# Retention and a squared-ReLU FFN in one kernel: transposing q and k two visits ahead of the scores

## The chip, the cores and the metric

The kernel runs on one core of a Trainium2 chip. The metric is the time on the device in microseconds (us), from the first to the last instruction, as the median of several runs. Five engines work beside each other, each with its own stream of instructions: TensorE (PE for its matmuls, PEld for its weight loads), VectorE (DVE), ScalarE (ACT), GpSimd (POOL) and SyncE (SP), whose stream here holds only transfers. What one engine needs from another it waits for at a semaphore.

## The reference

Two parts are computed, the second from the output of the first. In the retention part, each of 8 batches and 8 heads has 576 positions of 64 numbers. Scores of q against k are weighted by a decay that falls with the distance of two positions, later positions are masked away, and the result is multiplied by v. The FFN then takes 4608 tokens of 512 numbers through 2048 hidden ones.

```python
scores = scale * np.matmul(q, k.transpose(0, 1, 3, 2))       # (8, 8, 576, 576), scale = 1/8
gamma = 1.0 - 2.0 ** (-5.0 - np.arange(H))
rel = pos[:, None] - pos[None, :]
Dmat = np.where(rel >= 0, gamma[:, None, None] ** rel, 0.0)
attn = np.matmul(scores * Dmat, v)
x = attn.transpose(0, 2, 1, 3).reshape(4608, 512)
h = np.maximum(x @ w_in, 0.0)                                # (4608, 2048)
out = h * h @ w_out                                          # (4608, 512)
```

## The kernel before

The retention is done in 40 chunks: each batch has four of 128 positions and one of 64. Between chunks a state `u` is carried, so only scores within a chunk are formed. The FFN's matrix products are done by a scheme of seven products in place of eight (Strassen-Winograd): its sums are made by VectorE. Tokens go through the FFN in blocks of 512; one block is 28 steps (4 groups of hidden columns by 7 products), each of 8 matmuls. These steps are mixed with the chunks. At the end, after the last chunk, the second product of the FFN runs alone (line 893).

One turn of the main loop, a visit, works on two chunks at once: it forms the scores of chunk i and finishes the output of chunk i-1.

```python
for i in range(N_CH + 1):
    if i <= N_EARLY:                        # N_EARLY = 4: the start
        ...
        scale_q(i + 1, nc.gpsimd)
        if i < N_EARLY:
            ...
            turn(i + 1)
    else:
        if i == N_EARLY + 1:
            gone[0] = TOK
        if i + 1 < N_CH:
            scale_q(i + 1, nc.gpsimd)       # q times its decay, in place
        retain_a(i - 1)
        if i < N_TURN:                      # N_TURN = 9
            turn(i)                         # transposes on TensorE, the early chunks only
        ffn(i - 1, 0)                       # some FFN steps
        move(len(moves))                    # whatever copies are left
        if N_TURN <= i + 1 < N_CH:
            flip(i + 1)                     # transposes on VectorE
        retain_b(i - 1)
        if i < N_CH:
            scores(i)
        retain_c(i - 1)
        if N_TURN <= i + 1 < N_CH:
            spread(i + 1)                   # queues the copies of chunk i + 1
        ffn(i - 1, 1)                       # more FFN steps
    if i == 0:
        fetch_raw(2)
    if i + 3 < N_CH:
        load(i + 3)                         # q, k and v
    if 0 < i < N_EARLY:
        fetch_raw(1)
```

q and k come from memory with the position on the partition; the scores need the head's 64 numbers there. For chunks 9 to 39 this is done in two steps. `flip` transposes blocks of 32 by 32 on VectorE, once for k and once for q. `spread` puts 16 small copies (8 for a chunk of 64 positions) in a list, which ScalarE works off: they bring the blocks to their partitions. `move` issues copies from this list.

```python
def flip(i):
    cs = chunks[i][3]
    t = st[i]["flip"] = work2.tile([128, 4, 2, HP, 32], F32, tag="flip", name="flip")
    for j in (1, 0):
        nc.vector.transpose(t[:cs, :, j, :, :], loaded[i][j][:cs].rearrange("s (p e) (d a) -> s (e d) p a", e=2, d=2))  # L390

def spread(i):
    to = new_qk(i)
    for b in range(chunks[i][3] // 32):
        for g in range(4):
            moves.append(lambda b=b, g=g: nc.scalar.copy(          # L396
                to[32 * g:32 * g + 32, :, :, 32 * b:32 * b + 32], st[i]["flip"][32 * b:32 * b + 32, g, :, :, :]))

def scores(i):
    ...
    # 32 small matmuls of kT and qT into sc_ps: L433
    # VectorE: sc_ps times the mask, into the room of kT: L441
    # GpSimd: v times its decay, in place: L443

def scale_q(i, engine):
    ...
    engine.tensor_tensor(t, t, dv[...], op=ALU.mult)               # L373, in the place of q

def ffn(i, half):
    ...                                     # how many steps the tokens finished so far call for
    while steps and count:
        held[0] = half == 0 and count == 1
        move(3)                             # three copies ahead of each step
        step()
        count -= 1
```

An FFN step, as far as it is spoken of: step j of 7 adds into one of three banks of the accumulator memory, a, b or c.

```python
def ffn_in(n, mp, j):
    ...
    if j in OPENS:                          # 0, 1, 2
        sums[to] = ps_f.tile([128, 2, HT], F32, tag="f", name=f"h_{to}")     # three buffers
    ...                                     # 8 matmuls: L614
    if j == 0:
        nc.scalar.copy(p1, p)                                                # bank a, L624
    elif j == 1:
        nc.vector.tensor_tensor(u2, p, p1, op=ALU.add)                       # bank b, L626
    elif j == 2:
        nc.vector.tensor_tensor(p15, p, p1, op=ALU.add)                      # bank c, L628
    elif j == 3:
        nc.scalar.activation(g["A11"], p, AF.Relu)                           # bank a, L630
        nc.gpsimd.tensor_tensor(g["A11"], g["A11"], g["A11"], op=ALU.mult)   # L631
    elif j == 4:
        nc.vector.tensor_tensor(g["A22"], p, p15, op=ALU.add)                # bank b, L633
        square(g["A22"])                                                     # L621
    elif j == 5:
        nc.vector.tensor_tensor(g["S3"], p, u2, op=ALU.add)                  # bank c, L637
        square(g["S3"])
    else:
        nc.vector.tensor_tensor(g["A12"], p, p1, op=ALU.add)                 # bank b, L640
        square(g["A12"])
        queue.extend(g_sums(n, mp))                                          # four sums, L552 to L555, a transfer
```

The steps also work off, piece by piece, the conversion of the weights of the second product: five VectorE instructions (L207 to L225) and two of ScalarE (L215, L216) for each of 16 pieces, and sums over them.

Buffers: q has three, k and v have four, `flip` and `qk` have two each.

Of the kernel before, what the change touches and what calls it, by code (L numbers as in the profile page):

```python
# [9 lines left out]
F32 = mybir.dt.float32  # L10
# [5 lines left out]
C = 128  # L16
# [24 lines left out]
def kernel(  # L41
# [33 lines left out]
    nc = tc.nc  # L75
    ctx.enter_context(tc.manual_schedule())

    B, H, S, D = q.shape
    HP = H // 2
# [12 lines left out]
    N_CH = len(chunks)  # L92
# [5 lines left out]
    first = ExitStack()  # L98
    only = first.enter_context(tc.tile_pool(name="only", bufs=1))
    ld3 = first.enter_context(tc.tile_pool(name="ld3", bufs=3))  # L100
    ld4 = first.enter_context(tc.tile_pool(name="ld4", bufs=4))
    work = first.enter_context(tc.tile_pool(name="work", bufs=1))
    work2 = first.enter_context(tc.tile_pool(name="work2", bufs=2))
    ps_x = first.enter_context(tc.tile_pool(name="ps_x", bufs=1, space=PS))
    ps_t = first.enter_context(tc.tile_pool(name="ps_t", bufs=1, space=PS))
# [4 lines left out]
    W = [const.tile([128, N_MQ * NP * 128], F32, name=f"w{j}") for j in range(NP)]  # L110
# [17 lines left out]
    loaded = {}  # L128
    N_EARLY = TOK // C

    def load(i):
        b, ci, c0, cs = chunks[i]
        got = {name: pool.tile([128, H, D], F32, tag=name, name=f"{name}_ld") for name, pool in (("q", ld3), ("k", ld4), ("v", ld4))}
        if i == 0:
            nc.sync.dma_start(dv, decays)
        for name, src in (("q", q), ("k", k), ("v", v)):
            t = got[name]

            issue = nc.scalar if i == 0 and name != "q" else nc.sync
            at = src[b, :, c0:c0 + cs, :].rearrange("h s d -> s h d")  # L140
            if name == "v":
                issue.dma_start(t[:cs], at)
            else:

                issue.dma_start(t[:cs, 0:H // 2, :], at[:, 0:H // 2, :])
                for e in range(2):
                    issue.dma_start(t[:cs, H // 2 + e::2, :], at[:, H // 2 + 1 - e::2, :])
        loaded[i] = [got["q"], got["k"], got["v"]]

# [39 lines left out]
    def fetch_w(j):  # L191
        if j < len(pieces) and wide:
            nc.sync.dma_start(raw_of(j).bitcast(I64).rearrange("p (c f) -> p c f", c=N_DM), piece_src(j))
# [88 lines left out]
    def fetch_raw(count):  # L282

        for _ in range(count):
            if n_raw[0] < min(N_W1, n_made[0] + N_RAW):
                fetch_w(n_raw[0])
                n_raw[0] += 1
# [25 lines left out]
    def convert(count):  # L313
        for _ in range(count):
            f = next(w_in_steps, None)
            f and f()
# [1 line left out]
    dv = only.tile([128, H, 2 * NCH], F32, name="dv")  # L318
    exp_bias = const.tile([128, 1], F32, name="exp_bias")
    nc.gpsimd.memset(exp_bias, -896.0 * 2.0 ** 23)  # L320
    idle = only.tile([128, 128], F32, name="idle")
    nc.vector.memset(idle, 1.0)
    load(0)
    load(1)
    fetch_raw(1)
    load(2)

    ident = only.tile([128, 128], F32, name="ident")
    make_identity(nc, ident)

    msk = only.tile([128, 1, 1, CH], F32, name="msk")
# [1 line left out]
    for half in range(2):  # L333
        at = slice(CH * half, CH * half + CH)
# [8 lines left out]
    st = {i: {} for i in range(N_CH)}  # L343
# [11 lines left out]
    def rows(half, n=64):  # L355
        return slice(64 * half, 64 * half + n)
# [13 lines left out]
    def scale_q(i, engine):  # L370
        ci, cs = chunks[i][1], chunks[i][3]
        t = loaded[i][0][:cs]
        engine.tensor_tensor(t, t, dv[:cs, :, NCH + ci:NCH + ci + 1].to_broadcast([cs, H, D]), op=ALU.mult)  # L373
# [4 lines left out]
    N_TURN = 9  # L378
    moves = []

    def new_qk(i):
        t = work2.tile([128, 2, HP, C], F32, tag="qk", name="qk")
        st[i]["qT"], st[i]["kT"] = t[:, 0, :, :], t[:, 1, :, :]
        return t

# [4 lines that stand above are left out]
            nc.vector.transpose(t[:cs, :, j, :, :], loaded[i][j][:cs].rearrange("s (p e) (d a) -> s (e d) p a", e=2, d=2))  # L390

    def spread(i):
        to = new_qk(i)
        for b in range(chunks[i][3] // 32):
            for g in range(4):
                moves.append(lambda b=b, g=g: nc.scalar.copy(  # L396
                    to[32 * g:32 * g + 32, :, :, 32 * b:32 * b + 32], st[i]["flip"][32 * b:32 * b + 32, g, :, :, :]))

    def move(count):
        for f in moves[:count]:  # L400
            f()
        del moves[:count]

    def turn(i):

        cs = chunks[i][3]
        n_h = cs // CH
        p = ps_t.tile([128, 2, 512], F32, tag="t", name="t_ps").rearrange("p h (j d t) -> p h j d t", j=2, d=HP)
        for j in (1, 0):
            for hp in range(HP):  # L410
                for h in range(n_h):
                    nc.tensor.transpose(p[:, h, j, hp, :], loaded[i][j][rows(h), 2 * hp:2 * hp + 2, :],
                                        ident[rows(h), rows(h)])
        to = new_qk(i)[:, :, :, :cs].rearrange("p j d (h t) -> p j d h t", h=n_h)
        nc.scalar.copy(to[:, 1].rearrange("p d h t -> p h d t"), p[:, :n_h, 1, :, :])
        nc.vector.tensor_copy(to[:, 0].rearrange("p d h t -> p h d t"), p[:, :n_h, 0, :, :])
# [279 lines left out]
    def ffn(i, half):  # L696

        gone[0] += chunks[max(0, min(i, N_CH - 1))][3] / 2
        if steps and steps[0][0] == 0:

            move(6)
            for f in (step, lambda: convert(6)) if half else (lambda: convert(6), step):
                f()
            if half and steps and steps[0][0] == 0:
                step()
                convert(6)
            return
        if not behind:
            behind.append((gone[0] - HALF, done[0]))
        points = behind + [p for p in PACE if p[0] > behind[0][0]]  # L710
        want = points[-1][1]
        for (x0, y0), (x1, y1) in zip(points, points[1:]):
            if gone[0] < x1:
                want = y0 + (y1 - y0) * (gone[0] - x0) / (x1 - x0)
                break
        count = max(1, int(want) - done[0])
        while steps and count:
            held[0] = half == 0 and count == 1
            move(3)
            step()  # L720
            count -= 1
        held[0] = False
# [15 lines left out]
    for i in range(N_CH + 1):  # L738
        if i <= N_EARLY:

            if i == 1:
                convert(2)
            elif i == 2:
                convert(5)
            if i >= 1:
                retain_a(i - 1)
                if i < 3:
                    warm(4, False)
                else:
                    convert(1)  # L750
                    first_in(2 * i - 5, (0,))
                    convert(5)
                retain_b(i - 1)
                if i < 3:
                    warm(4, False)
                retain_c(i - 1)
            convert((0, 1, 1, 0, 1)[i])
            if i == N_EARLY:
# [3 lines that stand above are left out]
            if i == 2:  # L762
                convert(5)
                first_in(0, (0,))
            elif i == 3:
                convert(1)
                first_in(2, (0,))
                convert(5)
            elif i == N_EARLY:
                convert(5)  # L770
                step()
                convert(6)
            scale_q(i + 1, nc.gpsimd)
            if i < N_EARLY:
                if i < 2:
                    warm(6, False)
                turn(i + 1)
        else:
            if i == N_EARLY + 1:
                gone[0] = TOK  # L780
            if i + 1 < N_CH:
                scale_q(i + 1, nc.gpsimd)
            retain_a(i - 1)
            if i < N_TURN:
                turn(i)
            ffn(i - 1, 0)
            move(len(moves))
            if N_TURN <= i + 1 < N_CH:
                flip(i + 1)
            retain_b(i - 1)  # L790
            if i < N_CH:
                scores(i)
            retain_c(i - 1)
            if N_TURN <= i + 1 < N_CH:
                spread(i + 1)
            ffn(i - 1, 1)
        if i == 0:
            fetch_raw(2)
        if i + 3 < N_CH:
            load(i + 3)  # L800
        if 0 < i < N_EARLY:
            fetch_raw(1)
    assert n_next[0] == N_BLK
    first.close()

# [165 lines left out]
    for k in range(N_K + 1):  # L971
# [4 lines left out]
        for e in range(3):  # L976
# [8 lines left out]
            f = next(steps_0, None)  # L985
# [50 lines left out]
```

## Time and profile before

| what | value |
|---|---|
| median of 3 runs | 1007.1 us (1004.7 to 1008.47) |
| span of the profiled run | 1007.7 us |
| TensorE matmuls busy | 966.5 us, 96% |
| TensorE weight loads busy | 861.4 us, 85% |
| VectorE busy | 786.1 us, 78% |
| ScalarE busy | 351.3 us, 35% |
| GpSimd busy | 128.7 us, 13% |
| mean granted TensorE clock | 0.983 |

A busy time is the time in which at least one instruction of the engine was under way. A line such as L396 is a line of the kernel's code; a row of the profile gives the line, the engine, the operation, what is written and read, and how often. The idle time in front of an instruction is put down to the event that came last before it. The granted clock is given as a share of full speed. The chunks run until about 553 us, the FFN's remaining first-product steps until about 605 us, and the second product alone to the end.

### The profile page before, as it was taken

To read this page: it belongs to the slowest core of one execution; us is meant where nothing else is said; L and a number is where in the kernel's file an instruction comes from. 1 tells how busy PE (TensorE), PEld (TensorE's weight loads), DVE (VectorE), ACT (ScalarE), POOL (GpSimd) and SP (SyncE) were. 2 spreads that over 40 slices of the span, in tenths; PEclk is the share of its full clock that TensorE was granted. 3 is DMA by queue.
4 is the path that set the end of the run, shared out by engine and by line. 5 is a ranking of instruction groups with operands and counts; after the bars stand their busy time and mean duration, and the time that the engine had idled before them with its cause. 6 is when DMAs were issued, how large, how long until landed. Compare 5 with 4: busy or idle time off the path is not lost. (4 is left out here: it accounts for less than half of the span.)

```text
span 1007.7 us, 24117 instructions
## 1 busy us (share of the span) xinstructions
PE 966.5 (96%) x10092; PEld 861.4 (85%) x10092; DVE 786.1 (78%) x1458; ACT 351.3 (35%) x871; POOL 128.7 (13%) x121
## 2 busy tenths in 40 slices
PE   7899989999999899989989999999999999999998
PEld 6645768788878778877878889999999999999998
DVE  3789787768998799998977677777777677777766
ACT  3454575674665656746562110000000000000000
POOL 3211212312123131212120000000000000000000
PEclk7999999999999899999989999999999999999999
DMA  8883657655798589669437998684865757565351
GB/s 196 239 226 115 171 163 208 180 154 178 204 296 236 147 247 268 211 180 297 135 126 299 394 419 320 250 293 144 287 210 187 272 176 255 187 241 209 127 210 43
DMA packets 185037, 219.19 MB, mean 218 GB/s; under 512 B 118624, under 2 KB 135008, under 8 KB 175968
## 3 DMA queue, kind: packets, MB, share of 16 engines
q1 hardware_dynamic: 182816, 217.13, 66.3%
q8 instruction: 79, 1.29, 0.5%
q10 hardware_dynamic: 2112, 0.52, 0.2%
q14 instruction: 30, 0.25, 0.1%
HBM read 128.23 MB, written 89.39 MB: 216 GB/s over the span
## 5 line engine op out<-in xcount | busy, mean ns | idle before, releaser
L396 ACT COPY qk<-flip 32x256 f32<-32x256 f32 x440 | 177.1, 402 | 34.2 <-DVE flip L390 27.8
L614 PE MATMUL h_b<-room,w 128*128 128x256 f32 x736 | 179.4, 387 | 1.9 <-DVE room L539 1.6
L614 PEld LDWEIGHTS h_b<-room,w 128*128 128x128 f32 x736 | 139.6, 193 | 23.3 <-issue 2.1
L893 PE MATMUL o_b<-w,room 128*128 128x128 f32 x1168 | 144.5, 275 | 1.5 <-DVE room L844 1.5
L893 PEld LDWEIGHTS o_b<-w,room 128*128 128x128 f32 x1168 | 137.2, 192 | 1.7 <-DVE room L844 1.7
L893 PE MATMUL o_c<-w,room 128*128 128x128 f32 x1008 | 123.0, 275 | 0.0
L893 PEld LDWEIGHTS o_c<-w,room 128*128 128x128 f32 x1008 | 117.7, 192 | 0.0
L614 PE MATMUL h_c<-room,w 128*128 128x256 f32 x480 | 116.6, 386 | 0.0
L614 PE MATMUL h_a<-room,w 128*128 128x256 f32 x448 | 109.8, 389 | 3.1 <-ACT room L624 3.1
L907 ACT COPY r<-o_a 128x128 f32<-128x128 f32 x53 | 14.1, 265 | 273.3 <-PE o_a L893 242.5
L614 PEld LDWEIGHTS h_c<-room,w 128*128 128x128 f32 x480 | 91.8, 193 | 13.2
L614 PEld LDWEIGHTS h_a<-room,w 128*128 128x128 f32 x448 | 84.9, 193 | 15.7 <-ACT room L624 3.5
L893 PE MATMUL o_a<-w,a 128*128 128x128 f32 x688 | 85.6, 275 | 0.0
L631 POOL TENSOR_TENSOR room<-room 128x512 f32<-128x512 f32 x32 | 35.4, 1105 | 387.9 <-ACT room L630 368.5
L893 PEld LDWEIGHTS o_a<-w,a 128*128 128x128 f32 x688 | 81.2, 192 | 0.1
L621 DVE SCALAR_TENSOR_TENSOR room<-room 128x512 f32<-128x512 f32 x96 | 75.5, 786 | 3.3
L578 PE MATMUL h_ps<-room,w 128*128 128x512 f32 (+1 forms) x160 | 58.7, 515 | 3.5 <-DVE w L225 2.6
L373 POOL TENSOR_TENSOR q_ld<-q_ld,dv 128x512 f32<-128x512 f32 (+1 forms) x39 | 47.2, 1210 | 76.5 <-DMA q_ld<-in_q_dram 70.1
L455 PEld LDWEIGHTS x_ps<-qk,v_ld 64*64 64x64 f32 x1152 | 42.0, 141 | 15.3 <-issue 13.7
L433 PE MATMUL sc_ps<-qk 64*64 64x64 f32 x1152 | 35.5, 233 | 19.5 <-ACT qk L396 16.1
L455 PE MATMUL x_ps<-qk,v_ld 64*64 64x64 f32 x1152 | 51.1, 230 | 3.0 <-DVE qk L441 2.0
L633 DVE TENSOR_TENSOR room<-h_b,room 128x512 f32<-128x512 f32 x32 | 22.1, 690 | 39.0 <-PE h_b L614 38.9
(111 smaller groups left out, 1419.8 us busy)
## 6 DMA issues: line engine op xcount, KB each, us to landing
g_dram<-room SPq DMA_DIRECT2D x32, 1792.0 KB, 7.8
a<-g_dram SPq DMA_DIRECT2D x43, 1024.0 KB, 7.3
room<-g_dram SPq DMA_DIRECT2D x20, 1024.0 KB, 6.3
w<-w_dram SPq DMA_DIRECT2D x7, 1792.0 KB, 12.9
out_dram<-room SPq DMA_DIRECT2D x17, 512.0 KB, 3.3
w<-in_moe_w_in_dram SPq DMA_DIRECT2D x16, 512.0 KB, 5.7
w<-in_moe_w_out_dram SPq DMA_DIRECT2D x16, 512.0 KB, 3.8
v_ld<-in_v_dram SPq DMA_DIRECT2D x31, 256.0 KB, 4.0
```

The source lines that it names most:

```text
L373: engine.tensor_tensor(t, t, dv[:cs, :, NCH + ci:NCH + ci + 1].to_broadcast([cs, H, D]), op=ALU.mult)
L396: moves.append(lambda b=b, g=g: nc.scalar.copy(to[32 * g:32 * g + 32, :, :, 32 * b:32 * b + 32], st[i]["flip"][32 * b:32 * b + 32, g, :, : ...
L433: nc.tensor.matmul(sc[e][rows(h), hp, :], lhsT=kT[rows(e), hp, t], rhs=qT[rows(e), hp, t], start=True, stop=True, skip_group_check=True)
L455: own.append(lambda hp=hp, e=e, b=b: nc.tensor.matmul(x_at(hp, b, h), lhsT=s["vs"][rows(h), 2 * hp + b, :], rhs=s["ret"][rows(h), e, hp, : ...
L578: nc.tensor.matmul(p.rearrange("p h t -> p (h t)"), lhsT=w[:, c, :], rhs=xT[0][:, c, lo * HT:hi * HT], start=(c == 0), stop=(c == N_DM - 1))
L614: nc.tensor.matmul(p[:, mm, :], lhsT=w[:, c, :], rhs=xs[n][right][:, c, :], start=(j in OPENS and mm == 0 and c == 0), stop=(j in CLOSES a ...
L621: nc.vector.scalar_tensor_tensor(t, t, 0.0, t, op0=ALU.max, op1=ALU.mult)
L631: nc.gpsimd.tensor_tensor(g["A11"], g["A11"], g["A11"], op=ALU.mult)
L633: nc.vector.tensor_tensor(g["A22"], p, p15, op=ALU.add)
L893: nc.tensor.matmul(p, lhsT=s["lefts"][left][:, m, :], rhs=w_out[j][:, m, WO_SLOT[right], :], start=(i in OPENS and m == 0), stop=(i in CLO ...
L907: nc.scalar.copy(r[:, 0, 0:128], p)
```

## The change

The copies should no longer be issued close before the scores that need them, nor close behind the transposes that they read. So the whole chain is pulled apart: in visit i, q and k of chunk i+4 are loaded (v stays at i+3), GpSimd scales q of chunk i+3, VectorE transposes chunk i+2, and the copies of chunk i+1 are queued; what is left of the copies of chunk i is issued at the visit's start, ahead of the FFN steps instead of behind them. The transposes stand behind the scores and the mask of chunk i. The first chunks go over to the new order between visits 5 and 9.

This needs one more buffer of k (five) and one more of `qk` (three). Their room is found by letting two small constant tiles, `idle` and `ident`, lie in a part of the weight buffer `W[6]` that is not used at that time.

```diff
+    ld5 = first.enter_context(tc.tile_pool(name="ld5", bufs=5))
+    work3 = first.enter_context(tc.tile_pool(name="work3", bufs=3))
 ...
-    def load(i):
+    def load(i, names="qkv"):
 ...
-        for name, src in (("q", q), ("k", k), ("v", v)):
-            t = got[name]
+        got = loaded.setdefault(i, [None] * 3)
+        for name, pool, src in (("q", ld3, q), ("k", ld5, k), ("v", ld4, v)):
+            if name not in names:
+                continue
+            t = got["qkv".index(name)] = pool.tile([128, H, D], F32, tag=name, name=f"{name}_ld")
 ...
-    idle = only.tile([128, 128], F32, name="idle")
+    idle, ident = (W[6][:, at:at + 128] for at in (2688, 2816))
 ...
     def new_qk(i):
-        t = work2.tile([128, 2, HP, C], F32, tag="qk", name="qk")
+        t = work3.tile([128, 2, HP, C], F32, tag="qk", name="qk")
 ...
-    def move(count):
-        for f in moves[:count]:
-            f()
-        del moves[:count]
+    def move(count, i=N_CH):
+        while moves and count and moves[0][0] <= i:
+            nc.scalar.copy(*moves.pop(0)[1:])
+            count -= 1
 ...
-            if i + 1 < N_CH:
-                scale_q(i + 1, nc.gpsimd)
             retain_a(i - 1)
             if i < N_TURN:
                 turn(i)
+            move(C, i)
             ffn(i - 1, 0)
-            move(len(moves))
-            if N_TURN <= i + 1 < N_CH:
-                flip(i + 1)
             retain_b(i - 1)
             if i < N_CH:
                 scores(i)
             retain_c(i - 1)
             if N_TURN <= i + 1 < N_CH:
                 spread(i + 1)
+            if N_TURN <= i + 2 < N_CH:
+                flip(i + 2)
             ffn(i - 1, 1)
         if i == 0:
             fetch_raw(2)
-        if i + 3 < N_CH:
+        if i < N_TURN - 1:
             load(i + 3)
+        else:
+            if i == N_TURN - 1:
+                load(i + 3, "qk")
+            if i + 4 < N_CH:
+                load(i + 4, "qk")
+            if i + 3 < N_CH:
+                load(i + 3, "v")
         if 0 < i < N_EARLY:
             fetch_raw(1)
+        if i > N_EARLY:
+            for j in range(i + 1 + 2 * (i > N_EARLY + 1), min(i + 4, N_CH)):
+                scale_q(j, nc.gpsimd)
```

More of the change, by code (lines that the diff above doesn't have):

```diff
@@ L129 @@
     N_EARLY = TOK // C
-    def load(i):
+    def load(i, names="qkv"):
         b, ci, c0, cs = chunks[i]
-        got = {name: pool.tile([128, H, D], F32, tag=name, name=f"{name}_ld") for name, pool in (("q", ld3), ("k", ld4), ("v", ld4))}
         if i == 0:
             nc.sync.dma_start(dv, decays)
-        for name, src in (("q", q), ("k", k), ("v", v)):
-            t = got[name]
+        got = loaded.setdefault(i, [None] * 3)
[3 more added lines that the diff above has]
+            t = got["qkv".index(name)] = pool.tile([128, H, D], F32, tag=name, name=f"{name}_ld")
             issue = nc.scalar if i == 0 and name != "q" else nc.sync
@@ L147, in load @@
                     issue.dma_start(t[:cs, H // 2 + e::2, :], at[:, H // 2 + 1 - e::2, :])
-        loaded[i] = [got["q"], got["k"], got["v"]]
     pieces = [(0, m, e) for m in range(N_M) for e in range(2)]
@@ L326 @@
     load(2)
-    ident = only.tile([128, 128], F32, name="ident")
     make_identity(nc, ident)
@@ L392, in spread @@
     def spread(i):
-        to = new_qk(i)
+        t, to = st[i]["flip"], new_qk(i)
         for b in range(chunks[i][3] // 32):
             for g in range(4):
-                moves.append(lambda b=b, g=g: nc.scalar.copy(
-                    to[32 * g:32 * g + 32, :, :, 32 * b:32 * b + 32], st[i]["flip"][32 * b:32 * b + 32, g, :, :, :]))
-    def move(count):
-        for f in moves[:count]:
-            f()
-        del moves[:count]
+                moves.append((i, to[32 * g:32 * g + 32, :, :, 32 * b:32 * b + 32], t[32 * b:32 * b + 32, g, :, :, :]))
+    def move(count, i=N_CH):
+        while moves and count and moves[0][0] <= i:
+            nc.scalar.copy(*moves.pop(0)[1:])
+            count -= 1
     def turn(i):
```

## The prediction

> **What bounds the kernel now.** I read the busy rows first, then TensorE's own waits, then stretches of the time, and last the instructions around two of the waits. The page's busy rows:
>
> ```profile
> PE 966.5 (96%) x10092; PEld 861.4 (85%) x10092; DVE 786.1 (78%) x1458; ACT 351.3 (35%) x871; POOL 128.7 (13%) x121
> ...
> PEclk7999999999999899999989999999999999999999
> ```
>
> TensorE is the bound over the span: it lacks only 1007.7 - 966.5 = 41 us. The change can win only idle time of TensorE, or time at which its clock was lowered. The second line shows that the clock dips below full speed in a few slices of the middle. What TensorE waited for, in the whole span:
>
> ```profile
> PE sc_ps L433 <- ACT qk L396: 16.1, 19, 3.6
> PE sc_ps L433 <- DVE qk L416: 3.4, 3, 1.4
> PE h_a L614 <- ACT room L624: 3.1, 1, 3.1
> ...
> PE x_ps L455 <- DVE qk L441: 2.0, 1, 2.0
> PE h_b L614 <- DVE room L539: 1.6, 1, 1.6
> ```
>
> The columns are us in total, times and the longest. The largest entry is just what the change aims at: the scores (L433) waiting for ScalarE's copies (L396) of the transposed q and k, 16.1 us in 19 waits. By stretch (us, then busy time of each engine, granted clock, DMA):
>
> ```profile
> 120.00:240.00 120.00, 114.22 (x1423) 96.66 (x1422) 94.04 (x144) 73.70 (x181) 27.34 (x24) 0.99 0.63 178
> 240.00:510.00 270.00, 252.94 (x2930) 213.28 (x2928) 242.60 (x390) 164.59 (x392) 63.76 (x55) 0.97 0.73 221
> 510.00:600.00 90.00, 89.62 (x652) 77.56 (x651) 64.63 (x104) 21.53 (x49) 8.49 (x8) 0.98 0.78 304
> 600.00:1007.70 407.70, 402.85 (x3568) 401.39 (x3566) 299.84 (x679) 33.76 (x126) 1.04 (x1) 1.00 0.61 216
> ```
>
> TensorE's idle time where the changed code runs is 5.8 + 17.1 + 0.4 = 23 us, and the waits named above for this part (16.1 + 3.1 + 2.0 + 1.6) explain all of it. From 240 to 510 VectorE is busy 242.6 of 270 us, 90%: it is nearly a second bound. After 600 nothing of the change runs.
>
> The clock matters too. Two pairs of slices of 10 us around the longest waits, same columns:
>
> ```profile
> 320.00:330.00 10.00, 7.52 (x52) 6.16 (x50) 9.18 (x14) 8.52 (x20) 4.76 (x4) 0.94 0.99 263
> 330.00:340.00 10.00, 9.95 (x100) 8.31 (x101) 5.78 (x11) 5.37 (x15) 0.00 (x0) 0.72 0.48 120
> ...
> 500.00:510.00 10.00, 6.08 (x111) 5.07 (x109) 7.31 (x13) 5.46 (x13) 3.06 (x3) 0.82 0.47 177
> 510.00:520.00 10.00, 10.00 (x69) 8.29 (x68) 6.35 (x12) 6.46 (x16) 0.00 (x0) 0.84 0.03 10
> ```
>
> In slices of 1 us the clock is either 1.00 or 0.50. It is 0.50 for about 3.2 us from 138, 6.7 us from 329, 3.4 us from 438, 3.3 us from 476 and 6.4 us from 507, each time after TensorE had stood still for about 2 us or more. Half of these 23 us, less the part in which TensorE stood anyway, is about 11 us lost, beside the 23 us of idling.
>
> Why the copies are late is seen on ScalarE's own timeline (start, duration, instruction) at two of these places:
>
> ```profile
> 434.73 1.23 ACT L396 COPY qk<-flip 32x256 f32<-32x256 f32 x3 [5.67 <-DVE flip L390]
> 435.99 0.59 ACT L624 COPY room<-h_a 128x512 f32<-128x512 f32 x1
> ...
> 503.30 0.72 ACT L215 ACTIVATE w<-w,exp_bias 128x512 uint32<-128x512 uint32 x1 [2.66 <-DVE w L207]
> 503.93 0.65 ACT L216 ACTIVATE w<-w 128x512 f32<-128x512 uint32 x1
> 504.60 1.23 ACT L396 COPY qk<-flip 32x256 f32<-32x256 f32 x3
> 505.85 0.60 ACT L630 ACTIVATE room<-h_a 128x512 f32<-128x512 f32 x1
> 506.47 1.65 ACT L396 COPY qk<-flip 32x256 f32<-32x256 f32 x4
> ```
>
> At 434.7 ScalarE had stood 5.67 us for the transpose, which VectorE, running late, reached only then; the copy L624 queued behind it, and TensorE's next h_a waited 3.1 us for that. At 503.3 ScalarE stood for VectorE's weight conversion with seven copies still behind it in the queue, and the scores waited 3.6 us. ScalarE is only a third busy, so its rate is not the trouble: it inherits VectorE's lateness in order.
>
> **What the skill says.** The Trainium skill, "TensorE: Matmul & The Clock Gate", section on the HAM clock gate: the clock falls to half when the array has idled for about a window of 3.4 us, and needs about as long to come back. The trace agrees in the two levels and in the 3.2 to 6.7 us of half clock, but here 2.1 to 2.5 us of standing still were enough (before 138 and 329), while 1.6 us (at 297.5) was not. The same page, in its table and under "Architectural detail", says ScalarE and VectorE take their queues strictly in order; the two places above show it. "SBUF — State Buffer", section "Who interferes with whom": a VectorE instruction with two SBUF inputs and a GpSimd one that reads SBUF block each other. At 425.2 us VectorE's L539 took 1.54 us beside GpSimd's L373 of 1.50 us, against usual 0.68 and 1.06; so GpSimd's scaling isn't free to VectorE wherever it is put, but its amount does not change.
>
> **The change part by part.** No instruction of the steady part is added or removed: 31 chunks are still transposed by 62 VectorE instructions (0.70 and 0.66 us) and spread by 440 ScalarE copies of 0.402 us, and 40 scalings stay. What moves is order.
>
> (1) The transpose of chunk i+1 stood in visit i after the first half of the FFN steps, and its copies followed right behind retain_c, about 1.7 us of TensorE's time later (304.6 to 306.3 us in one visit of the timeline). Now it is issued a whole visit earlier, and a visit lasts about (540 - 100)/31 = 14 us. ScalarE should hardly ever stand for it: the 27.8 us (15 times) that it stood for L390 go, and with them the 3.1 us of h_a.
>
> (2) The last of the 16 copies were dealt out in threes among the FFN steps before the scores. Now the remainder is flushed ahead of those steps: half a visit, some 3.5 steps of 8 x 0.236 = 1.89 us, so 6.6 us of margin. The longest wait was 3.6 us, so I expect at most 1 of the 16.1 us to stay.
>
> (3) VectorE's mask (L441) now stands ahead of the transposes instead of behind: 1.36 us earlier. Of the 2.0 us wait I give it 1.
>
> (4) With no wait above 2 us left of this kind, most of the half clock goes: 9 of 11 us.
>
> Gains: 15 + 2.6 + 1 + 9 = 27.6 us.
>
> (5) Given back: from 240 to 510 TensorE without these losses (17 us idle, about 9 us clock) would need 244 us. VectorE has 390 instructions there. Where it is saturated (17 to 19 instructions in 9.9 us) one takes some 0.57 us, that is 222 us; by its busy time it needs 243. So it would be 91 to nearly 100% loaded, and the FFN's tightest link lets it lag only about one step (bank b is read after step 4 and written again in step 6). I put 6 us of new waits there, clock included.
>
> (6) The flush puts up to 7 x 0.402 = 2.8 us of copies ahead of one FFN copy per visit: 1 us in all, since that copy has two steps (3.8 us) of room.
>
> (7) The switch from one scheme to the other: chunks 9 and 10 are loaded only in the visits before they are transposed, and VectorE stands in order for load, scaling and transpose. Landing takes up to 10.3 us for q and GpSimd waited 60 us for q before 120 us. 1.5 us.
>
> Net: 27.6 - 8.5 = 19 us, 1007 - 19 = **988 us**.
>
> **Rivals.** *VectorE becomes the bound*: 390 instructions in 270 us speak for it, and its idle time there is only 27 us, 14 of it waiting for h_b (L633). Then the 26 us of TensorE's losses there shrink to perhaps 8 recovered, plus 5 before 240: about 994 to 997. Against it speaks that in the kernel before, at 90%, TensorE waited for VectorE's FFN work only 1.8 us. *Everything is recovered*: 23 + 11 us, at no cost: 973; for it that VectorE's instructions overlap when dense (starts 0.60 us apart for 0.68 us). *The transfer takes the wait's place*: transposes in order behind q that hasn't landed would stop VectorE and so everything; the time would be 1005 to 1015. In the steady part a load now has about two visits (28 us) against 10.3 us, and before, GpSimd's wait for q from 230 to 520 was 4.6 us, once; so this is only a start-up cost.
>
> **Range and chances.** The middle lies between the first two rivals, nearer to the balance of (1) to (7). 979 is two thirds of full recovery plus a little luck with the clock; 1000 is VectorE taking most of it. The 2% line is 987 us, close to the middle: faster by over 2% 0.43, within 2% 0.54, slower by over 2% 0.03.
>
> **What would show it.** Right: the scores' wait for L396 under 2 us, ScalarE's wait for L390 near zero, no half clock between 240 and 510, TensorE's busy share of that phase near 97%, VectorE's near 95% with its waits for h_b shrunk, and new small waits of h_b and h_c for VectorE. Wrong: VectorE idle for flip's inputs (q_ld) beyond visit 10, or new waits of TensorE for VectorE above 12 us with fresh half-clock stretches. If the clock doesn't recover though the waits go, part (4) is wrong.

## The result and the profile after

| what | before | changed |
|---|---|---|
| median | 1006.99 us | 996.49 us (993.29 to 998.64) |
| ratio | | 0.9895, 95% interval 0.9862 to 0.9928 |
| span of the profiled run | 1007.7 us | 994.4 us |
| TensorE's waits, 120 to 600 us | 23.4 us | 16.8 us |
| clock below full, 120 to 600 us | 11.9 us | 6.8 us |

The change brings 10.5 us, 1.05%; 19 us were predicted. The last row adds up, over slices of 10 us, the share of the clock that was missing, as full-clock time; 1.1 us of the 11.9 and 0.7 us of the 6.8 fell while TensorE stood, so those count in both rows.

The page of the changed kernel; lines are numbered anew (L403 is L396 of before, L616 is L614, L635 is L633):

```profile
PE 960.5 (97%) x10092; PEld 855.8 (86%) x10092; DVE 788.7 (79%) x1458; ACT 350.2 (35%) x871; POOL 131.9 (13%) x121
...
L616 PE MATMUL h_b<-room,w 128*128 128x256 f32 x736 | 181.9, 391 | 10.6 <-DVE room L635 4.3
L403 ACT COPY qk<-flip 32x256 f32<-32x256 f32 x440 | 177.0, 402 | 6.3
```

The same 440 copies take the same 177 us, but ScalarE stood only 6.3 us in front of them and none of it for a transpose. In front of the FFN's matmuls into bank b, TensorE now stood 10.6 us, for VectorE. Its waits from 120 to 600 us (total, times, longest) in the changed kernel:

```profile
PE h_b L616 <- DVE room L635: 4.0, 3, 1.4
PE sc_ps L435 <- ACT qk L403: 3.5, 6, 1.1
PE h_b L616 <- DVE room L628: 3.5, 1, 3.5
PE x_ps L457 <- ACT u_sb L495: 3.1, 4, 2.1
PE h_b L616 <- DVE room L541: 1.6, 1, 1.6
PE x_ps L457 <- DVE qk L443: 0.8, 1, 0.8
```

The wait that the change is for went from 16.1 to 3.5 us, and the 3.1 us for bank a are gone. New are 7.5 us for L635 and L628, which read FFN sums out of bank b, and 3.1 us (0.4 before) for L495: a copy of two numbers per partition on ScalarE at the end of retain_b, behind which retain_c's first matmul must stand. The stretches:

```profile
120.00:240.00 120.00, 117.15 (x1444) 98.58 (x1442) 99.30 (x153) 73.64 (x182) 28.89 (x25) 1.00 0.64 175
240.00:510.00 270.00, 256.27 (x2984) 215.93 (x2984) 248.36 (x395) 171.00 (x411) 64.11 (x54) 0.97 0.73 219
510.00:600.00 90.00, 89.63 (x649) 78.57 (x648) 66.58 (x103) 14.41 (x32) 9.98 (x9) 1.00 0.90 348
```

VectorE is now busy 248 of 270 us in the middle, 92%, with 395 instructions in place of 390. The clock there is 0.97 as before.

What a new wait looks like: VectorE of the changed kernel (start, duration, instruction) around the longest.

```profile
424.92 0.68 DVE L443 TENSOR_TENSOR qk<-sc_ps,msk 128x512 f32<-128x512 f32 x1
425.52 0.69 DVE L392 STREAM_TRANSPOSE flip<-k_ld 64x512 f32<-64x512 f32 x1
426.14 0.66 DVE L392 STREAM_TRANSPOSE flip<-q_ld 64x512 f32<-64x512 f32 x1
426.74 0.64 DVE L543 TENSOR_TENSOR room<-room 128x512 f32<-128x512 f32 x1
427.31 0.67 DVE L555 TENSOR_TENSOR room<-room 128x512 f32<-128x512 f32 x1
427.90 1.25 DVE L247 TENSOR_TENSOR w<-w,w 128x256 f32<-128x256 f32 x1
429.19 1.17 DVE L248 TENSOR_TENSOR w<-w,w 128x256 f32<-128x256 f32 x1
430.28 0.68 DVE L628 TENSOR_TENSOR room<-h_b,room 128x512 f32<-128x512 f32 x1
```

VectorE has no gap: mask, transposes, a sum over x, an FFN sum, two sums over weights, and only then L628, for which TensorE had been ready since about 427.5. L247 and L248 took 1.25 and 1.17 us instead of about 0.42 (the median of their eight executions each at this shape). GpSimd in the same microseconds, changed kernel:

```profile
427.67 1.21 POOL L633 TENSOR_TENSOR room<-room 128x512 f32<-128x512 f32 x1 [8.48 <-ACT room L632]
428.84 1.23 POOL L375 TENSOR_TENSOR q_ld<-q_ld,dv 128x512 f32<-128x512 f32 x1
430.04 1.23 POOL L445 TENSOR_TENSOR v_ld<-v_ld,dv 128x512 f32<-128x512 f32 x1
```

The Trainium skill's "SBUF — State Buffer", section "Who interferes with whom", says that a VectorE instruction with two SBUF inputs and a GpSimd instruction that reads SBUF block each other. The two slow VectorE sums agree: they have two such inputs and stand beside these three instructions. TensorE in slices of 1 us (us, busy, clock, DMA) shows the price of the wait:

```profile
428.00:429.00 1.00, 0.00 (x0) 1.00 0.00 0
429.00:430.00 1.00, 0.00 (x0) 0.80 0.00 0
430.00:431.00 1.00, 0.00 (x0) 0.50 0.00 0
431.00:432.00 1.00, 0.99 (x2) 0.50 0.00 0
432.00:433.00 1.00, 1.00 (x4) 0.50 0.00 0
433.00:434.00 1.00, 1.00 (x4) 0.50 0.00 0
434.00:435.00 1.00, 1.00 (x3) 0.50 0.40 152
```

After 3.5 us of standing it runs at half clock: 3 or 4 matmuls touch a slice; at full clock, from 437 to 439 us, 6 do. The slice from 430 to 440 us has a mean clock of 0.68, so this lasts until about 436.4: 5.4 us of running at half speed, 2.7 us lost.

The profiled spans differ by 13.3 us, the medians by 10.5. The profiled execution of the kernel before took 1009.39 us, more than any of its four runs. Part of the excess lies at the start, where nothing of the new order runs yet: between 10 and 20 us the profiled run of before had a granted clock of 0.59, that of the changed kernel 1.00, and its chunk 4 was masked at 46.2 instead of 48.0 us. The rest of the difference about adds up: 6.6 us less waiting and 5.1 us less missing clock, 0.4 us of it counted twice.

### The profile page after: what moved, and what is told of

Read it like the earlier page. It is cut to its first block, busy times and chain, and to the rows that moved or that the text cites. A ratio compares the mean times of both kernels' runs of the same rounds, so it can differ in the third digit from the quotient of the medians.

```text
span 994.4 us, 24115 instructions
## 1 busy us (share of the span) xinstructions
PE 960.5 (97%) x10092; PEld 855.8 (86%) x10092; DVE 788.7 (79%) x1458; ACT 350.2 (35%) x871; POOL 131.9 (13%) x121
## 5 line engine op out<-in xcount | busy, mean ns | idle before, releaser
L616 PE MATMUL h_b<-room,w 128*128 128x256 f32 x736 | 181.9, 391 | 10.6 <-DVE room L635 4.3
L403 ACT COPY qk<-flip 32x256 f32<-32x256 f32 x440 | 177.0, 402 | 6.3
L616 PEld LDWEIGHTS h_b<-room,w 128*128 128x128 f32 x736 | 139.9, 193 | 33.2 <-DVE room L635 6.1
L616 PE MATMUL h_c<-room,w 128*128 128x256 f32 x480 | 115.9, 385 | 0.0
L917 ACT COPY r<-o_a 128x128 f32<-128x128 f32 x53 | 14.1, 266 | 272.5 <-PE o_a L903 241.9
L616 PE MATMUL h_a<-room,w 128*128 128x256 f32 x448 | 107.6, 383 | 0.0
L616 PEld LDWEIGHTS h_c<-room,w 128*128 128x128 f32 x480 | 91.9, 193 | 13.6 <-DVE room L642 0.3
L616 PEld LDWEIGHTS h_a<-room,w 128*128 128x128 f32 x448 | 83.7, 190 | 12.1 <-ACT room L626 0.3
L633 POOL TENSOR_TENSOR room<-room 128x512 f32<-128x512 f32 x32 | 36.9, 1152 | 370.4 <-ACT room L632 264.5
L623 DVE SCALAR_TENSOR_TENSOR room<-room 128x512 f32<-128x512 f32 x96 | 72.3, 753 | 3.3
L580 PEld LDWEIGHTS h_ps<-room,w 128*128 128x128 f32 x160 | 29.2, 190 | 25.0 <-issue 20.4
L445 POOL TENSOR_TENSOR v_ld<-v_ld,dv 128x512 f32<-128x512 f32 (+1 forms) x40 | 47.5, 1187 | 13.6 <-DMA v_ld<-in_v_dram 5.9
```

What stands on the lines that cost most here:

```text
L403: nc.scalar.copy(*moves.pop(0)[1:])
L445: nc.gpsimd.tensor_tensor(vs[:cs], vs[:cs], dv[:cs, :, ci:ci + 1].to_broadcast([cs, H, D]), op=ALU.mult)
L580: nc.tensor.matmul(p.rearrange("p h t -> p (h t)"), lhsT=w[:, c, :], rhs=xT[0][:, c, lo * HT:hi * HT], start=(c == 0), stop=(c == N_DM - 1))
L616: nc.tensor.matmul(p[:, mm, :], lhsT=w[:, c, :], rhs=xs[n][right][:, c, :], start=(j in OPENS and mm == 0 and c == 0), stop=(j in CLOSES a ...
L623: nc.vector.scalar_tensor_tensor(t, t, 0.0, t, op0=ALU.max, op1=ALU.mult)
L917: nc.scalar.copy(r[:, 0, 0:128], p)
```

## Experiments

Theory: ScalarE's copies were late because, in order, ScalarE inherits VectorE's lateness; the change frees the scores of that, and TensorE then meets VectorE itself, which has too little slack to give 19 us. Rivals: one of the two moves (transposes earlier, copies earlier) does it all and the other is idle; or what is left comes from ScalarE's order or from transfers, not from VectorE's load. All ratios are to the kernel before, with their 95% intervals; that of the changed kernel is 0.9895. Each edit is one to the changed kernel unless said otherwise. Waits come from one profiled execution of a kernel, which can lie some us off the median (996.09 us for the changed kernel, 1006.11 for e2, 998.83 for e9, 994.78 for e11).

### The two moves apart

e1_flush_only, an edit to the kernel before:

```diff
+            move(len(moves))
             ffn(i - 1, 0)
-            move(len(moves))
```

> The kernel before with one part of the change: what is left of the copies is issued ahead of the first half of the FFN steps instead of behind it; transposes, loads and scaling stay where they were. Theory A (copies are late because ScalarE stands for late transposes and conversions of VectorE; margin before the scores is what counts): the scores' wait for the copies falls from 16 us to about 5 us, but ScalarE's wait for the transposes (27.8 us) stays and pushes the FFN copy of bank a, so TensorE's wait for that one stays at 3 us or grows; time 999 to 1003 us. Rival B (only the distance between transpose and copies counts): nothing gained, 1005 to 1009 us.

e2_flip_only:

```diff
-            move(C, i)
             ffn(i - 1, 0)
+            move(C, i)
```

> The changed kernel with one part undone: what is left of the copies is issued behind the first half of the FFN steps again, as before; transposes stay two visits ahead. Theory A: ScalarE hardly waits for transposes, but the scores still come close behind the last copies, which queue behind weight conversions: the scores' wait is 6 to 9 us and the time 999 to 1003 us. Rival B (distance from the transposes is all): as the changed kernel, 995 to 998 us, with the scores' wait at 4 us or less.

Measured: copies early alone 1000.65 us, ratio 0.9942 (0.9922 to 0.9961); transposes early alone 1002.35 us, 0.9964 (0.9949 to 0.9979). TensorE's and then ScalarE's waits with the copies early alone:

```profile
PE sc_ps L433 <- ACT qk L396: 6.0, 7, 2.2
...
PE h_a L614 <- ACT room L624: 2.7, 2, 2.5
```

```profile
ACT qk L396 <- DVE flip L390: 38.7, 18, 5.1
```

and the same two with the transposes early alone:

```profile
PE sc_ps L435 <- ACT qk L403: 15.6, 19, 4.7
```

```profile
ACT w L218 <- DVE w L210: 14.6, 9, 3.8
```

```profile
500.19 0.72 ACT L218 ACTIVATE w<-w,exp_bias 128x512 uint32<-128x512 uint32 x1 [3.84 <-DVE w L210]
```

With the copies early alone the scores wait 10 us less, but ScalarE stands longer for the transposes (27.8 before, 38.7 now) and the FFN's bank a still waits. With the transposes early alone ScalarE never stands for them, yet the scores wait as long as before, since the copies still come last and queue behind the weight conversion L218, which stands 14.6 us for VectorE: at 500.19 us it had stood 3.84 us with seven copies behind it, and there the scores waited 4.7 us. So rival B falls: the distance from the transposes alone leaves the scores' wait where it was. Theory A had that wait too small as well, at 6 to 9 us; the time is as it had it. Each move alone is worth 0.4 to 0.6%, together 1.05%: about a sum.

### VectorE lightened, in both kernels

e3_light_before (in the kernel before) and e4_light_after (in the changed kernel) leave out 32 of VectorE's instructions of the second weight's conversion, so the second weights have neither their exponent nor their sign:

```diff
+        if j >= N_W1:
+            four = five = lambda: None
         return [one, two, beside, three, four, five]
```

> The kernel before with VectorE lightened: two of five VectorE instructions of each of the 16 pieces of the second weight's conversion are left out (scaling by the exponent and the sign), 32 instructions, about 25 us of VectorE, nearly all between 240 and 510 us; the second weights are then not converted rightly. Theory (in the changed kernel VectorE is the new bound, in the kernel before ScalarE's late copies are): the kernel before gains only through less lateness of VectorE, about 3 to 8 us: 999 to 1004 us. Rival (VectorE isn't a bound in either): under 3 us.

> The changed kernel with the same 32 VectorE instructions left out. Theory (VectorE is the new bound): TensorE's direct waits for VectorE between 120 and 600 us fall from 10 us to under 4 us, stretches of half clock go too, and the time falls by 8 to 13 us, to 983 to 988 us, more than what the kernel before gains from the same cut. Rival (what is left are late copies on ScalarE and transfers, not VectorE): less than 4 us gained, 993 to 997 us.

Measured: the kernel before gains 5.9 us, to 1001.31 (0.9946, 0.9928 to 0.9965), the changed one 11.7 us, to 984.83 (0.9777, 0.9761 to 0.9792). Stretch and waits of the lightened changed kernel:

```profile
240.00:510.00 270.00, 260.82 (x3078) 220.85 (x3077) 237.07 (x383) 174.76 (x420) 60.46 (x54) 1.00 0.76 228
```

```profile
PE sc_ps L437 <- ACT qk L405: 2.8, 4, 1.1
PE h_b L618 <- DVE room L637: 2.7, 2, 1.5
PE x_ps L459 <- ACT u_sb L497: 2.1, 4, 1.2
PE h_b L618 <- DVE room L543: 1.6, 1, 1.6
...
PE h_c L618 <- DVE room L632: 0.5, 1, 0.5
```

The scores' wait in the lightened kernel before:

```profile
PE sc_ps L435 <- ACT qk L398: 14.7, 17, 2.4
```

The same cut is worth twice as much once the copies are out of the way, and the clock stays full from 120 to 600 us. In the lightened kernel before, the scores still wait 14.7 us for the copies and the clock still lacks 11.9 us: there ScalarE's order is the limit, which less VectorE work doesn't cure. The direct waits for VectorE fell from 10.2 to 4.8 us, where under 4 were expected; a wait of 1.3 us in the second product, which here begins before 600 us, is not in the 4.8. That VectorE's load is what the changed kernel runs into is shown by this pair.

### The order of VectorE's work

e5_dealt_flips:

```diff
-            nc.vector.transpose(t[...], loaded[i][j][...])
+            later.append(lambda j=j, src=loaded[i][j]: nc.vector.transpose(t[...], src[...]))
 ...
             move(3)
             step()
+            if later:
+                later.pop(0)()
 ...
             retain_c(i - 1)
+            while later:
+                later.pop(0)()
```

> The changed kernel with the two transposes of a visit dealt out: one behind each of the next two FFN steps instead of both at once behind the mask; VectorE's work is the same, only its bursts are shorter. Theory (VectorE's total load limits, and bursts make it bite): TensorE's direct waits for VectorE fall from 10 us to 6 to 8 us; time 991 to 995 us. Rival (only the total load counts, the order of VectorE's work does not): 995 to 998 us.

e7_mask_behind:

```diff
+            if N_TURN <= i + 2 < N_CH:
+                flip(i + 2)
             retain_b(i - 1)
             if i < N_CH:
                 scores(i)
             retain_c(i - 1)
 ...
-            if N_TURN <= i + 2 < N_CH:
-                flip(i + 2)
```

> The changed kernel with the transposes ahead of retain_b, the scores and the mask again, where they stood before, but still two visits ahead. If the mask's place matters as the prediction's part (3) says, TensorE's wait for the mask (0.8 us) rises by 1 to 2 us and the time to 997 to 999 us; if it doesn't, 995 to 998 us, the same as the changed kernel.

Measured: dealt out 1000.09 us, 0.9944 (0.9924 to 0.9964), a miss for both theories, as its median is 3.6 us above that of the changed kernel, though the two intervals just overlap; mask behind 999.09 us, 0.9924 (0.9900 to 0.9948), whose interval overlaps that of the changed kernel. With dealt-out transposes TensorE's direct waits for VectorE rose from 11.5 to 12.8 us (from 100 to 600 us) and that for the tiny copy from 3.1 to 4.7 us. Shorter bursts don't help here. A likely reason, not shown, is that VectorE has hardly a gap to put them in, so that a transpose between two steps delays the next read-out of a bank as well. With the mask behind, TensorE's wait for it is 2.5 us in place of 0.8, as part (3) has it.

### GpSimd's share

e8_no_scaling leaves GpSimd's scaling of q out for chunks 10 to 39, so their scores lack the decay by position:

```diff
-                scale_q(j, nc.gpsimd)
+                if j <= N_TURN:
+                    scale_q(j, nc.gpsimd)
```

> The changed kernel without GpSimd's scaling of q for chunks 10 to 39 (30 instructions of 1.2 us left out; the scores of these chunks lack the decay). VectorE's instruction count is the same. If instructions of VectorE with two inputs are held up by GpSimd's, VectorE's busy time for the same work falls by up to 10 us, its waits with it, and the time is 990 to 994 us; if GpSimd's work costs VectorE nothing, 995 to 998 us.

Measured: 991.68 us, 0.9857 (0.9829 to 0.9885). From 240 to 510 us, VectorE's instructions add up to 272.5 us in 395 in the changed kernel (0.690 us each) and 270.1 us in 405 here (0.667 each): the same 405 at 0.690 would be 279 us, so about 9 us of VectorE's time there went with GpSimd's scaling of q. Most of it shows in rows whose two inputs lie in SBUF, as here (changed kernel, then e8):

```profile
L554 DVE TENSOR_TENSOR room<-room 128x512 f32<-128x512 f32 x17 | 13.4, 786 | 0.0
...
L554 DVE TENSOR_TENSOR room<-room 128x512 f32<-128x512 f32 x17 | 11.6, 684 | 0.0
```

L635, which reads one of its inputs from a bank, took 687 and 686 ns, and the transposes of k 696 and 697. Taking the scaling away is worth about 5 us, with intervals that overlap in part.

### Work moved to ScalarE

e6_a12_scalar moves one of three squares per group to ScalarE, as a ReLU and a square one step later; e9_early_fence puts retain_b and the tiny copy one FFN step earlier; e10_fence_a12 has both; e12_fence_a12_late issues the square another step later; e11_fence_a11 has the early tiny copy and moves GpSimd's square to ScalarE.

```diff
             nc.vector.tensor_tensor(g["A12"], p, p1, op=ALU.add)
-            square(g["A12"])
-            queue.extend(g_sums(n, mp))
+            todo = g_sums(n, mp)
+            second, t = todo[1], g["A12"]      # e12: todo[2]
+            def with_square():
+                second()
+                nc.scalar.activation(t, t, AF.Relu)
+                nc.scalar.activation(t, t, AF.Square)
+            todo[1] = with_square              # e12: todo[2]
+            queue.extend(todo)
```

```diff
-            ffn(i - 1, 0)
-            retain_b(i - 1)
+            early = [lambda: retain_b(i - 1)]
+            ffn(i - 1, 0, early)               # issued ahead of the last step of this half
+            while early:
+                early.pop()()
```

```diff
-            nc.gpsimd.tensor_tensor(g["A11"], g["A11"], g["A11"], op=ALU.mult)
+            nc.scalar.activation(g["A11"], g["A11"], AF.Square)
```

> The changed kernel with one of the three squares per group of FFN steps moved from VectorE (0.6 to 0.8 us) to two ScalarE instructions (about 1.2 us), dealt out one step later; 32 squares, some 17 of them between 240 and 510 us, so about 11 us less of VectorE there and 20 us more of ScalarE, which has 99 us free. Theory (VectorE is the bound): 988 to 992 us. Rival (ScalarE's queue in order is as tight as VectorE): the gain is eaten by later copies, the scores' wait rises over 6 us, 995 to 1000 us.

> The changed kernel with retain_b, and the tiny ScalarE copy behind it that retain_c waits for, one FFN step earlier, ahead of the last step of the first half; the rest is unchanged. In the changed kernel TensorE waited 3.1 us for that copy, in the kernel with one square on ScalarE 7.8 us. Theory (it is ScalarE's order that costs here): this wait falls below 1 us and the time to 991 to 994 us. Rival (TensorE then merely meets VectorE's lateness one step later): 995 to 998 us.

> The early tiny copy together with one square per group moved from VectorE to ScalarE. Theory (VectorE's load is the bound, and the moved square lost its gain only at the tiny copy): 986 to 991 us, TensorE's waits for VectorE under 6 us and for the tiny copy under 1 us. Rival (ScalarE's queue in order costs as much elsewhere, at the copies for the scores): 995 to 1000 us.

> The early tiny copy together with GpSimd's square (one per group) moved to ScalarE, right behind the ReLU that it follows. VectorE's own work is the same, GpSimd loses about 17 of 54 instructions between 240 and 510 us. If GpSimd's reads hold up VectorE's instructions with two inputs, VectorE's busy time falls by 3 to 5 us there and the time to 989 to 992 us; if not, or if ScalarE's 0.6 us more per group cost as much, it is as with the early copy alone.

> The early tiny copy together with one square per group on ScalarE, the square issued one FFN step later still. In the kernel with the square one step earlier ScalarE stood 5.9 us for VectorE's sum that the square reads (990 to 995 us measured there). Theory (ScalarE's standing in order for VectorE is what is left of that kernel's loss): ScalarE's wait for that sum falls below 2 us, the waits for the tiny copy and the copies for the scores fall from 6.4 to under 4 us, 988 to 992 us. Rival (VectorE's last sum of the group, which reads the square, now has to wait for ScalarE and takes the gain back): VectorE waits for the square for 3 us or more, 992 to 996 us.

| run | us | ratio (95% interval) | waits for VectorE | for the tiny copy | for the copies of q and k |
|---|---|---|---|---|---|
| changed kernel | 996.49 | 0.9895 (0.9862 to 0.9928) | 10.2 | 3.1 | 3.5 |
| e6, square on ScalarE | 999.47 | 0.9937 (0.9914 to 0.9960) | 4.3 | 7.8 | 4.8 |
| e9, early tiny copy | 995.35 | 0.9888 (0.9866 to 0.9910) | 9.5 | 1.5 | 2.7 |
| e10, both | 992.65 | 0.9861 (0.9838 to 0.9883) | 4.0 | 2.7 | 3.7 |
| e12, both, square later | 993.00 | 0.9866 (0.9845 to 0.9887) | 4.2 | 2.4 | 2.6 |
| e11, early tiny copy, GpSimd's square | 998.65 | 0.9909 (0.9890 to 0.9929) | 4.0 | 4.7 | 3.2 |

The last three columns are TensorE's waits in us from 120 to 600 us. e6 came out in its rival's range: VectorE's waits shrank as they should, but ScalarE's queue grew and its next link gave way: not so much the copies for the scores, as the rival had it, as the tiny copy:

```profile
PE x_ps L457 <- ACT u_sb L495: 7.8, 7, 2.9
PE sc_ps L435 <- ACT qk L403: 4.8, 8, 1.1
```

The early tiny copy alone does little, since VectorE's waits stay, as e9's rival had it. Together they give 992.65 us. The prediction for e10 was 986 to 991. In e12 ScalarE no longer stood for the sum that the square reads (5.9 us in e10), and VectorE's last sum of the group waited only 0.7 us for the square; yet the time is the same, so that standing had cost nothing. What both have against them is at another place: VectorE's L628, which adds a copy that ScalarE makes, stood 11.4 us for ScalarE in e10 and 11.7 in e12, 2.2 in the changed kernel; what that cost was not tested. In e11 VectorE's mean instruction was 0.684 us against 0.690, so these squares had hardly held VectorE up, and the wait for the tiny copy was 4.7 us. TensorE's waits for VectorE fell to 4.0 us in its profiled execution, but that was the fastest of the five, and its median is above that of e9, within the intervals.

Two versions thus stand at 993 us, below both kernels; their intervals overlap that of the changed kernel a little, so a gain over it of 3 to 4 us is likely, not certain.

## Why the prediction was right, and where its size was not

- **The whole.** The range of 979 to 1000 us held (its lower end takes back 28 of the 34 us, four fifths and not the two thirds that it is called); the middle was 8.5 us too fast. Of the signs that were named for being right, ScalarE no longer stood for the transposes, TensorE had new waits for VectorE (one of them 3.5 us long), and VectorE was 92% busy, near the 95 named. The others did not come: the scores waited 3.5 us and not under 2, three stretches of half clock stand between 240 and 510 us, and TensorE was busy 95% there and not 97. Fresh half clock was named as a sign of being wrong, together with new waits for VectorE above 12 us; these were 7.6.
- **Parts (1) and (3), right.** ScalarE's 27.8 us for the transposes and TensorE's 3.1 us for bank a (the sum counts 2.6 of them and does not say why) are gone, and the mask's wait fell from 2.0 to 0.8 us. e1 shows that without (1) both of the first remain.
- **Part (2), right in kind.** 3.5 us stayed, 1 was expected. e2 shows that this part does most for the scores: without it they wait 15.6 us, with it alone (e1) 6.0.
- **Part (4), right for the old waits.** 9 of 11 us of half clock were to come back; of what the old kind of wait cost, 1.7 us are left, after two waits of together 0.7 us in the scores near 254 us. But the new waits lower the clock too: 2.7 us lost after the 3.5 us wait for L628 and 1.7 after the 2.1 us wait for the tiny copy. They belong to part (5). In e4 the clock lost nothing.
- **Part (5), the term that was mis-sized.** "I put 6 us of new waits there, clock included." In the profiles the new waits are 7.6 us for VectorE's read-outs (L635, L628, L639: 7.8, against 0.2 before), 2.7 us more for the tiny copy, and 4.4 us of clock behind these, 14.7 us in all. The whole balance from the two profiles: gains of 12.6 us at the scores, 3.1 at bank a, 1.2 at the mask and 9.1 of clock while TensorE worked (10.8 before, 1.7 left) are 26.0 us, where 27.6 were predicted. Less 14.7, where 8.5 were predicted for all costs, this is 11.3. The spans differ by 13.3 us, of which 1.8 were won by chunk 4. The upper end of the prediction's range for VectorE's load, 91 to nearly 100%, is the one that fits: as the changed kernel is busy 248.36 us with 395 instructions, 390 take about 245 us, an estimate, against 244 us of TensorE. The lower end came from stretches in which VectorE was full, and in these GpSimd was idle. Two slices of the kernel before (VectorE's column is the third behind the width, GpSimd's the fifth):

```profile
420.00:430.00 10.00, 10.00 (x164) 8.43 (x163) 9.21 (x12) 6.41 (x16) 3.97 (x3) 1.00 0.79 261
430.00:440.00 10.00, 6.91 (x57) 5.27 (x55) 9.90 (x19) 5.10 (x13) 0.00 (x0) 0.90 0.18 53
```

  Beside GpSimd 12 instructions fill 9.21 us, without it 19 fill 9.90. In the whole stretch GpSimd's scaling of q alone costs VectorE some 9 us of 270 (e8). That was so before the change too, where L539 took 1.54 us beside it. The rival "VectorE becomes the bound" had 994 to 997 us; 996.5 came.
- **Part (6)** can't be told apart. No wait for bank a appeared; but the copies now stand in one block, and the tiny copy, in the same queue, was not on the list at all. e9 shows that moving it alone is worth some 1 us, within the intervals; e6 shows that the wait for it becomes the main one as soon as ScalarE has more to do.
- **Part (7), about nothing.** VectorE stood 1.5 us for k, once, near 85 us. Chunk 10 was masked at 125.8 instead of 128.0 us, 2.2 us earlier, and chunk 4 had already been 1.8 us earlier.
- What stays open: why dealing the transposes out costs 3.6 us in the median. The named waits grew by 1.3 + 1.6 = 2.9 us, but its profiled run lost less clock. And how much of the scatter of 5 us between runs of one kernel is the clock's. The fastest run of the changed kernel, 993.29 us, had the highest mean clock, 0.998, and the slowest, 998.64, the lowest, 0.991; but in e4 the fastest run, 983.11 us, had the lowest, 0.994.

## What to carry to other kernels

A wait for an engine that is only a third busy need not be its own, as ScalarE's 27.8 us of standing for VectorE show: ask for whom it stood, in order, before it. When such a wait is taken from the path, work out the load of the engine behind it at the new, shorter time, with its instructions at the length they have beside their neighbours; here, at 90% and more, only a third of the 34 us of standing and slow clock came back. A wait of 2.1 us on TensorE cost 1.7 us more in clock, so a few new long waits can eat much of what was won.

## What was not expected of the hardware

The half clock needs less standing still than the window of 3.4 us in the Trainium skill's "TensorE: Matmul & The Clock Gate", section on the HAM clock gate: here it began 2.1 us after TensorE had come to a stop at 427.5 us, and, near 255.5 us, after two stops of 0.2 and 0.5 us with a few short matmuls between. At 497.9 us it began only 1.1 us after a stop of 2.1 us was over. The measurement decides. In slices of 1 us, each of the eight stretches of half clock in the two profiles, from 120 to 600 us, lasted about 3.4 us or about 6.8 us. And two VectorE instructions of 128x256 took 1.25 and 1.17 us beside GpSimd's, in place of 0.42: nearly three times as long.
